# The scale of a finished stage and its first two splits placed ahead of the weights' steps of its last unit

## Chip, cores and metric

One Trainium2 chip, one of its cores. The metric is the device time of one execution in microseconds; three executions of the kernel before took 1237.06, 1237.91 and 1239.82 us, median 1237.91.

## What is computed

Attention over 4 batches and 12 heads (448 tokens, head size 64), whose output, 1792 tokens of 768 features, goes through two feed-forward blocks:

```python
q_n, k_n = rmsnorm(q, g_q), rmsnorm(k, g_k)
attn = softmax(scale * q_n @ k_n.T)
x = attn @ v                       # as [1792, 768]
x = (x @ w_a) * (x @ w_b) @ w_out  # 768 -> 1536 -> 768
h = x @ w_in                       # 768 -> 2048
out = (max(h, 0) + alpha * min(h, 0)) @ w_out2
```

All inputs are f32 drawn from a normal distribution; w_a, w_b, w_out and w_in, w_out2 are the weights of the two blocks.

## The kernel before

The batches go through four stages each: `a` (both products of the first block and their elementwise product `ab`), `y` (its output), `h` (the first product of the second block, with its activation) and `o` (the output). The stages are emitted in a fixed order: a0 y0 h0 o0 a1 y1 a2 h1 o1 y2 a3 h2 y3 o2 h3 o3. Every f32 operand of a product is split into two f16 parts, hi and lo, after a scaling by a power of two; a product is three matmuls (hi hi, hi lo, lo hi), `prod`. A stage is a run of units. A unit is one chain of matmuls against one weight tile of 128 columns: a stage `a` has 24 units of 18 matmuls (6 k-tiles), `y` 12 of 18, `h` 16 of 18, `o` 24 of 12. Between the units a stage yields, and steps of the attention of later batches are emitted there, at a rate for each stage.

The weights of the first batch are prepared while they are first used, in units numbered along the stream of the stages (a0 is 0 to 23, y0 24 to 35, h0 36 to 51, o0 52 to 75). `next_w` (L735), called once for each unit u, gives out what is due then by `advance` (L722) and the list `STEPS` (L714): the load of unit u + 10 (`w_load`, a DMA on SP's queue, L629), the convert of u + 8 (`w_convert`: L645 on ACT, L648 and L651 on DVE, the squares L659 on ACT), the scale of u + 6 (`w_scale`: a total over the partitions on PE by a matmul with ones, L123, then small columns on DVE by `power`, L110: L115, L118, L121) and the split of u + 3 (`w_split`: hi by L706 on ACT, lo by L707 on DVE, and a store to a scratch tensor in HBM, L710). From a1 on the split weights are only loaded back from the scratch tensor, four units ahead (L625). `next_w` also takes one task of the list `tasks` if there is any.

At the end of a stage `a` the last `ab` (L783 on DVE, read from the chain's PSUM tile) is squared on ACT with its sum (L786); a total on PE over all twelve sums, a reduction on DVE (L131) and `power` give the scale `sab`; then the twelve `ab` tiles are split with it (`split`, L759: hi by L761 on ACT, lo by L762 on DVE). A stage `y` ends alike: the last y tile is copied out on ACT (L821) and squared (L822), six `norm` matmuls with a matrix of ones add the squares, a maximum on DVE (L830) and `power` give `sy`, and six tiles are split. Where the next stage uses these tiles (a0, a1, and y0), the splits are emitted at once; elsewhere (a2, a3, y1, y2, y3) they are put on the list `tasks`, one for each following unit. `after` (L803) decides that.

The program's order is not the order on the engines. A scheduler of the framework places every instruction on its engine's queue before the run: among the instructions that it takes to be ready it prefers the one that was emitted earlier. The queues themselves run in order on the chip.

PSUM tiles named `x` (totals, `norm`, the attention's output `x`) share one buffer. The attention's own instructions that stand near the ends of the stages are L418 (maximum of scores), L431, L435 (exponent), L450, L480 and L481 (probabilities split), L531 and L532 (output split), L386 and L387 (values split).

Of the kernel before, what the change touches and what calls it, by code (L numbers as in the profile page):

```python
# [19 lines left out]
def attention_gated_mlps_kernel(  # L20
# [19 lines left out]
    KD, KF, KF2 = DM // 128, DF // 128, DF2 // 128  # L40
# [28 lines left out]
    def slot32(name):  # L69
        return slot_p.tile([128, S], F32, tag="slot", name=name)  # L70
# [36 lines left out]
    def mm(o, a, b, first, last):  # L107
        nc.tensor.matmul(out=o, lhsT=a, rhs=b, start=first, stop=last)  # L108

    def power(total, s, i):  # L110


        n = total.shape[1]
        h = sm_p.tile([128, 4], I32, tag="pw", name="pw")[:, 0:n]
        nc.vector.tensor_scalar(  # L115
            h, total.bitcast(I32), 1, 0x7F800000, op0=ALU.logical_shift_right, op1=ALU.bitwise_and
        )
        nc.vector.tensor_scalar(  # L118
            s.bitcast(I32), h, -1.0, float(205 << 23), op0=ALU.mult, op1=ALU.add
        )  # L120
        nc.vector.tensor_scalar(i.bitcast(I32), h, 1.0, float(49 << 23), op0=ALU.mult, op1=ALU.add)  # L121

    def total(cols, n, groups=1):  # L123

        ps = ps_x.tile([128, 512], F32, tag="x", name="tot")
        p = cols.shape[0]
        mm(ps[:, 0:n], ones[:p], cols, True, True)
        if n == groups:
            return ps[:, 0:n]
        t = sm_p.tile([128, 4], F32, tag="tot", name="tots")[:, 0:groups]  # L130
        nc.vector.reduce_sum(  # L131
            out=t, in_=ps[:, 0:n].rearrange("p (g k) -> p g k", g=groups), axis=AX.X
        )
        return t
# [476 lines left out]
    for st in stages:  # L611
        n, parts, _ = CHAINS[st[0]]
# [84 lines left out]
    def junk(width, n):  # L697
        return one_p.tile([128, width], BF16, tag="junk", name="junk")[:, 0:n]
# [23 lines left out]
    def advance(u):  # L722

        for todo, steps, done in ((firsts, STEPS, at[0]), (again, AGAIN, at[1])):
            for i, (f, ahead) in enumerate(steps):
                while done[i] < (done[i - 1] if i else len(todo)):
                    x = todo[done[i]]
                    if x > u + ahead or (f is w_split and x not in scales):
                        break
                    f(x)  # L730
                    done[i] += 1
# [3 lines left out]
    def next_w():  # L735
        u = cur[0]
        cur[0] += 1
        w16.pop(u)
        advance(u)
        if tasks:  # L740
            tasks.pop(0)()

    def unit():
        w = w16[cur[0]]
        return w.rearrange("p l (k f) -> p l k f", f=128)

    def prod(o, w, kk, x, first, last):
        hi, lo = w[:, 0, kk, :], w[:, 1, kk, :]
        mm(o, hi, x[:, 0], first, False)
        mm(o, hi, x[:, 1], False, False)  # L750
        mm(o, lo, x[:, 0], False, last)

    def new_ps():
        return ps_m.tile([128, 512], F32, tag="p", name="p")

    def tmp():
        return tmp_p.tile([128, S], F32, tag="t", name="t")

    def split(t, s, name):  # L759
        x = slot(name)  # L760
        nc.scalar.activation(out=x[:, 0], in_=t, func=AF.Copy, scale=s)  # L761
        nc.vector.scalar_tensor_tensor(  # L762
            out=x[:, 1], in0=t, scalar=s, in1=x[:, 0], op0=ALU.mult, op1=ALU.subtract
        )
        return x

    def stage_a(b):
        raw = {}
        for f in range(KF):
            for w in range(2):  # L770
                yield
                ps = new_ps()[:, 0:S]
                hw = unit()
                for kk in range(KD):
                    prod(ps, hw, kk, X[b, kk], kk == 0, kk == KD - 1)
                i = inv["a"][:, 2 * f + w:2 * f + w + 1]
                next_w()
                if w == 0:
                    t = tmp()
                    nc.scalar.activation(out=t, in_=ps, func=AF.Copy, scale=i)  # L780
                else:
                    raw[f] = ab = slot32(f"ab32_{b}_{f}")
                    nc.vector.scalar_tensor_tensor(  # L783
                        out=ab, in0=ps, scalar=i, in1=t, op0=ALU.mult, op1=ALU.mult
                    )
                    nc.scalar.activation(  # L786
                        out=junk(768, S), in_=ab, func=AF.Square,
                        accum_out=ssab[:, b % 2, f:f + 1],
                    )
        for kk in range(KD):  # L790
            X.pop((b, kk))
        power(total(ssab[:, b % 2], KF), sab[:, b:b + 1], iab[:, b:b + 1])

        def one(f):
            AB[b, f] = split(raw.pop(f), sab[:, b:b + 1], f"ab{b}_{f}")

        after(stages_after("a", b) == "y", one, KF)

    def stages_after(kind, b):
        i = stages.index(f"{kind}{b}")  # L800
        return stages[i + 1][0] if i + 1 < len(stages) and stages[i + 1][1] == str(b) else ""

    def after(now, one, n):  # L803
        if now:
            for i in range(n):
                one(i)
        else:
            tasks.extend((lambda i=i: one(i)) for i in range(n))

    def stage_y(b):  # L810
        raw, sq = {}, [slot_p.tile([128, 2, S], BF16, tag="slot", name=f"sq{b}_{i}") for i in range(KD // 2)]
        for m in range(KD):
            ps = new_ps()[:, 0:S]
            for kh in range(2):
                yield
                hw = unit()
                for kk in range(KD):
                    prod(ps, hw, kk, AB[b, kh * KD + kk], kh + kk == 0, kh == 1 and kk == KD - 1)
                if kh == 1:
                    raw[m] = t = slot32(f"y32_{b}_{m}")  # L820
                    nc.scalar.activation(out=t, in_=ps, func=AF.Copy, scale=inv["y"][:, m:m + 1])  # L821
                    nc.scalar.activation(out=sq[m // 2][:, m % 2], in_=t, func=AF.Square)  # L822
                next_w()
        for f in range(KF):
            AB.pop((b, f))
        ps = ps_x.tile([128, 512], F32, tag="x", name="norm")[:, 0:S]
        for m in range(KD):
            mm(ps, onesb, sq[m // 2][:, m % 2], m == 0, m == KD - 1)
        t = sm_p.tile([128, 1], F32, tag="mx", name="mx")
        nc.vector.tensor_reduce(out=t, in_=ps, axis=AX.X, op=ALU.max)  # L830
        power(t, sy[:, b:b + 1], iy[:, b:b + 1])

        def one(m):
            Y[b, m] = split(raw.pop(m), sy[:, b:b + 1], f"y{b}_{m}")

        after(stages_after("y", b) == "h", one, KD)

    def stage_h(b):
        raw = {}
# [79 lines left out]
    if True:  # L919
# [18 lines left out]
        n, done = 0, 0  # L938
# [18 lines left out]
        for i, st in enumerate(stages):  # L957
            s, b = st[0], int(st[1])
            if s == "a":
                while done < (b + 1) * NP:  # L960
                    step()
            n, parts, _ = CHAINS[s]
            ticks = n * parts
            gen = {"a": stage_a, "y": stage_y, "h": stage_h, "o": stage_o}[s](b)
            want, acc = 3 * RATE.get(st, 0), 0
            for _ in gen:
                acc += want
                while acc >= ticks:
                    acc -= ticks
                    step()  # L970
# [30 lines left out]
```

## Time and profile before

| | |
|---|---|
| median of 3 executions | 1237.91 us |
| profiled execution, its time | 1242.48 us |
| profiled execution, its span | 1240.7 us |
| mean granted TensorE clock | 0.981 |
| busy share of the span: PE, DVE, ACT, POOL | 94%, 55%, 60%, 1% |
| end of the last chain of a0, start of the first of y0 | 214.7 and 224.0 us |
| end of the last chain of y0, start of the first of h0 | 275.8 and 288.0 us |
| stretch read for h0, for o0 | 288 to 354 us, 354 to 444 us |

Times in the rows are microseconds from the start of the span. PE is TensorE's matmuls, whose ends are modelled; DVE is VectorE, ACT is ScalarE, SPq the DMA issues of SyncE. The first matmul of y0 comes 9.3 us after the last one of a0, the first of h0 12.2 us after the last one of y0; between them PE runs totals, `norm` and scores of the attention.

### The profile page before, as it was taken

Reading aid. Unit: us, or ns where it says so; the run is one execution under the profiler, and the core shown is the slowest. Engines: PE = TensorE matmul, PEld = TensorE weight load, DVE = VectorE, ACT = ScalarE, POOL = GpSimd, SP = SyncE. Lnnn points to the kernel's source line nnn. Section 1 sums busy time; section 2 is a strip of 40 time slices with the busy share of each in tenths; the row PEclk is TensorE's granted clock in tenths of the full one; section 3 lists DMA queues with packets and bytes.
Section 4 is the critical chain, followed back from the end, with each engine's and each line's share of the span. In section 5 each row is a group of like instructions: output and inputs, shape, how many; then the busy total and the mean of one; then the engine's idle time right before and its main releaser. Section 6 shows DMA issues by size and latency. Waiting matters only on the chain.

```text
span 1240.7 us, 18165 instructions
## 1 busy us (share of the span) xinstructions
PE 1169.5 (94%) x6574; PEld 598.9 (48%) x6574; DVE 679.8 (55%) x1455; ACT 740.8 (60%) x1504; POOL 9.2 (1%) x32
## 2 busy tenths in 40 slices
PE   6897998889999799989999999999999999999998
PEld 3553554444444444434455454545555555555554
DVE  7988998979999766677651466332111440102400
ACT  6998999989999966677642465543311441213311
POOL 1000000000000000000000000000000000000000
PEclk9997999897999999999999999999999999999999
DMA  6546999999999999987953737876333333344343
GB/s 185 172 139 184 287 323 306 297 277 306 302 269 300 268 258 243 228 189 183 213 160 115 177 117 164 187 190 164 102 115 115 115 115 110 106 143 131 98 126 90
DMA packets 311242, 234.67 MB, mean 189 GB/s; under 512 B 175440, under 2 KB 284496, under 8 KB 311152
## 3 DMA queue, kind: packets, MB, share of 16 engines
q1 hardware_dynamic: 311040, 233.43, 71.2%
q8 instruction: 52, 0.85, 0.3%
q0 software_dynamic: 112, 0.07, 0.1%
q14 instruction: 38, 0.31, 0.1%
HBM read 155.79 MB, written 32.24 MB: 152 GB/s over the span
## 4 chain that ended last, share of the span: by engine, by line
PE 53%; ACT 1%; DMA 1%; DVE 0%; issue 0%; SPq 0%; ACTq 0%
PE p L108 48%; PE s L108 2%; PE x L108 2%; DMA pT<-p 1%; PE p L884 1%; ACT t L877 0%; ACT pf L435 0%; PE norm L108 0%; ACT p L480 0%; DVE nm L418 0%; SPq L487 0%; DVE p L481 0%; ACT x L531 0%; PE tot L108 0%; DVE v L387 0%
## 5 line engine op out<-in xcount | busy, mean ns | idle before, releaser
L108 PEld LDWEIGHTS <-w 128*128 128x128 f16 x4896 | 475.9, 99 | 473.3 <-issue 45.3
L108 PE MATMUL p<-x,w 128*128 128x448 f16 x1728 | 335.9, 353 | 2.8 <-ACT t L780 2.0
L108 PE MATMUL p<-g,w 128*128 128x448 f16 x1152 | 230.0, 356 | 5.8 <-ACT w L706 2.5
L108 PE MATMUL p<-y,w 128*128 128x448 f16 x1152 | 223.3, 355 | 0.0
L108 PE MATMUL p<-ab,w 128*128 128x448 f16 x864 | 169.6, 356 | 1.7 <-ACT ab L761 1.6
L418 DVE TENSOR_REDUCE nm<-s 128x2 f32<-128x896 f32 x84 | 91.0, 1085 | 38.0 <-PE s L108 37.6
L480 ACT ACTIVATE p<-pf,ri 128x448 f16<-128x448 f32 x126 | 81.8, 663 | 35.3 <-DMA pT<-p 27.6
L108 PE MATMUL s<-kT,qT 128*64 128x448 f16 (+1 forms) x336 | 89.2, 433 | 14.1 <-ACT pf L435 10.3
L481 DVE SCALAR_TENSOR_TENSOR p<-pf,ri,p 128x448 f16<-128x448 f32 x126 | 84.4, 681 | 32.9 <-ACT p L480 32.7
L435 ACT ACTIVATE pf<-s,nm,esc 128x448 f32<-128x448 f32 x126 | 90.0, 718 | 1.3
L859 DVE SCALAR_TENSOR_TENSOR t<-t,al,p 128x448 f32<-128x448 f32 x55 | 37.3, 678 | 95.0 <-ACT t L858 95.0
L783 DVE SCALAR_TENSOR_TENSOR ab<-p,inv_a,t 128x448 f32<-128x448 f32 x48 | 32.6, 678 | 95.5 <-PE p L108 95.4
L707 DVE SCALAR_TENSOR_TENSOR w<-wf,sc,w 128x768 f16<-128x768 f32 (+1 forms) x76 | 70.0, 928 | 5.6 <-ACT w L706 5.3
L877 ACT ACTIVATE t<-p,inv_o 128x448 f32<-128x448 f32 x24 | 25.5, 1063 | 77.3 <-PE p L108 77.3
L645 ACT ACTIVATE wf<-raw 128x768 f32<-128x768 f32 (+1 forms) x76 | 63.1, 831 | 13.0 <-DMA raw<-in_moe_w_in_dram 5.4
L786 ACT ACTIVATE junk<-ab 128x448 bf16<-128x448 f32 x48 | 27.4, 571 | 68.1 <-DVE ab L783 68.0
L651 DVE SCALAR_TENSOR_TENSOR wf<-raw,wf 128x768 int32<-128x768 int32 (+1 forms) x76 | 66.0, 869 | 0.4
L706 ACT ACTIVATE w<-wf,sc 128x768 f16<-128x768 f32 (+1 forms) x76 | 65.0, 863 | 0.7 <-issue 0.7
L659 ACT ACTIVATE junk<-wf 128x768 bf16<-128x768 f32 (+1 forms) x76 | 58.9, 775 | 4.1 <-DVE sc L118 1.2
L858 ACT ACTIVATE t<-p 128x448 f32<-128x448 f32 x55 | 29.8, 541 | 46.8 <-PE p L108 46.4
L844 ACT ACTIVATE g<-t,cgf 128x448 f16<-128x448 f32 x55 | 36.7, 668 | 34.6 <-DVE t L859 34.6
L845 DVE SCALAR_TENSOR_TENSOR g<-t,cgf,g 128x448 f16<-128x448 f32 x55 | 37.5, 682 | 29.5 <-ACT g L844 29.5
(139 smaller groups left out, 1029.1 us busy)
## 6 DMA issues: line engine op xcount, KB each, us to landing
w<-sc_a SPq DMA_DIRECT2D x72, 384.0 KB, 3.1
w<-sc_h SPq DMA_DIRECT2D x48, 384.0 KB, 3.0
w<-sc_o SPq DMA_DIRECT2D x72, 256.0 KB, 3.1
w<-sc_y SPq DMA_DIRECT2D x36, 384.0 KB, 3.1
raw<-in_moe_w_in_dram SPq DMA_DIRECT2D x16, 768.0 KB, 7.3
raw<-in_moe_w_out_dram SPq DMA_DIRECT2D x24, 512.0 KB, 5.5
raw<-in_moe_w_a_dram SPq DMA_DIRECT2D x12, 768.0 KB, 7.0
raw<-in_moe_w_b_dram SPq DMA_DIRECT2D x12, 768.0 KB, 6.5
```

Of the source, the lines that this page charges most:

```text
L108: nc.tensor.matmul(out=o, lhsT=a, rhs=b, start=first, stop=last)
L418: nc.vector.tensor_reduce(out=nm, in_=ps[:, :, 0:S], axis=AX.X, op=ALU.max, negate=True)
L435: nc.scalar.activation(out=pf, in_=ps[:, j, 0:S], func=AF.Exp, bias=nm[:, j:j + 1], scale=scale[j], accum_out=su[:, j:j + 1],)
L480: nc.scalar.activation(out=t[:, 0, :, 0:KP], in_=pf, func=AF.Copy, scale=r)
L481: nc.vector.scalar_tensor_tensor(out=t[:, 1, :, 0:KP], in0=pf, scalar=r, in1=t[:, 0, :, 0:KP], op0=ALU.mult, op1=ALU.subtract,)
L645: nc.scalar.activation(out=t, in_=hi.bitcast(F32), func=AF.Prelu, scale=2.0 ** -112, alpha=-(2.0 ** 32))
L651: nc.vector.scalar_tensor_tensor(out=ti, in0=lo, scalar=29, in1=ti, op0=ALU.logical_shift_right, op1=ALU.bitwise_or)
L659: nc.scalar.activation(out=junk(768, size(kind)), in_=t, func=AF.Square, accum_out=sums[0][:, j:j + 1])
L706: nc.scalar.activation(out=w[:, 0], in_=t, func=AF.Copy, scale=s)
L707: nc.vector.scalar_tensor_tensor(out=w[:, 1], in0=t, scalar=s, in1=w[:, 0], op0=ALU.mult, op1=ALU.subtract)
L845: nc.vector.scalar_tensor_tensor(out=x[:, 1], in0=t, scalar=cgf[:, f:f + 1], in1=x[:, 0], op0=ALU.mult, op1=ALU.subtract,)
L859: nc.vector.scalar_tensor_tensor(out=t, in0=t, scalar=al[:, f:f + 1], in1=ps, op0=ALU.mult, op1=ALU.add)
```

## The change

The last `next_w` of the stages `a` and `y` is no longer called after the unit's matmuls (in `a` that was ahead of the eviction of `ab`, in `y` behind the eviction and square of the last tile) but from `after`, that is behind the total and the scale. Where the splits are emitted at once, it is called between the second and the third of them; where they become tasks, just ahead of queueing them. The number of calls is the same, and no instruction is added or removed.

```diff
@@ stage_a
                 i = inv["a"][:, 2 * f + w:2 * f + w + 1]
-                next_w()
+                if f < KF - 1 or w == 0:
+                    next_w()
                 if w == 0:
...
-        after(stages_after("a", b) == "y", one, KF)
+        after(stages_after("a", b) == "y", one, KF, next_w)
@@
-    def after(now, one, n):
+    def after(now, one, n, last):
+
         if now:
             for i in range(n):
+                if i == 2:
+                    last()
                 one(i)
         else:
+            last()
             tasks.extend((lambda i=i: one(i)) for i in range(n))
@@ stage_y
                     nc.scalar.activation(out=sq[m // 2][:, m % 2], in_=t, func=AF.Square)
-                next_w()
+                if m < KD - 1 or kh == 0:
+                    next_w()
...
-        after(stages_after("y", b) == "h", one, KD)
+        after(stages_after("y", b) == "h", one, KD, next_w)
```

## Rows read from the trace of the kernel before

**Rows 1.** Stretches: start:end, length, busy us of each engine (instructions), granted clock, DMA.
```profile
214.70:224.00 9.30, 3.26 (x23) 2.15 (x23) 8.81 (x24) 8.15 (x17) 0.19 (x1) 0.84 0.99 223
...
275.80:288.00 12.20, 6.66 (x27) 2.65 (x27) 10.41 (x32) 9.71 (x22) 0.44 (x1) 0.63 1.15 333
288.00:354.00 66.00, 65.12 (x358) 32.87 (x358) 62.74 (x124) 61.78 (x123) 1.02 (x3) 0.96 1.08 297
354.00:444.00 90.00, 78.18 (x448) 37.59 (x447) 74.35 (x167) 78.46 (x170) 0.00 (x0) 0.96 1.10 275
```

**Rows 2.** Timeline of PE, a0 to y0: start, us, instruction, [idle before <-releaser].
```profile
211.17 3.58 PE L108 MATMUL p<-x,w 128*128 128x448 f16 x18
...
221.00 0.60 PE L108 MATMUL tot<-ssab,ones 128*128 128x12 f32 x2 [2.76 <-ACT junk L786]
...
224.03 1.28 PE L108 MATMUL p<-ab,w 128*128 128x448 f16 x3 [1.57 <-ACT ab L761]
```

**Rows 3.** Timeline of DVE, end of a0.
```profile
216.08 1.01 DVE L707 SCALAR_TENSOR_TENSOR w<-wf,sc,w 128x768 f16<-128x768 f32 x1
...
217.67 0.55 DVE L648 TENSOR_SCALAR wf<-wf 128x768 int32<-128x768 int32 x1
...
218.25 0.96 DVE L651 SCALAR_TENSOR_TENSOR wf<-raw,wf 128x768 int32<-128x768 int32 x1
...
219.20 0.68 DVE L783 SCALAR_TENSOR_TENSOR ab<-p,inv_a,t 128x448 f32<-128x448 f32 x1
```

**Rows 4.** Timeline of ACT, end of a0.
```profile
218.26 0.67 ACT L480 ACTIVATE p<-pf,ri 128x448 f16<-128x448 f32 x1 [0.16 <-DMA pT<-p]
...
219.31 0.84 ACT L659 ACTIVATE junk<-wf 128x768 bf16<-128x768 f32 x1 [0.38 <-DVE tots L131]
...
220.28 0.58 ACT L786 ACTIVATE junk<-ab 128x448 bf16<-128x448 f32 x1
...
222.34 0.89 ACT L645 ACTIVATE wf<-raw 128x768 f32<-128x768 f32 x1 [0.58 <-DMA raw<-in_moe_w_out_dram]
...
223.32 6.81 ACT L761 ACTIVATE ab<-ab,sab 128x448 f16<-128x448 f32 x12
```

**Rows 5.** Timeline of PE, y0 to h0.
```profile
279.30 0.58 PE L108 MATMUL tot<-ss,ones 128*128 128x2 f32 x2 [2.80 <-ACT junk L659]
...
280.69 2.42 PE L108 MATMUL norm<-sq,onesb 128*128 128x448 bf16 x6
...
287.48 0.58 PE L108 MATMUL tot<-ss,ones 128*128 128x2 f32 x2 [2.73 <-ACT junk L659]
```

**Rows 6.** Timeline of DVE, end of y0.
```profile
283.15 0.62 DVE L830 TENSOR_REDUCE mx<-norm 128x1 f32<-128x448 f32 x1 [0.40 <-PE norm L108]
...
284.82 0.55 DVE L648 TENSOR_SCALAR wf<-wf 128x768 int32<-128x768 int32 x1
...
285.39 0.15 DVE L115 TENSOR_SCALAR pw<-mx 128x1 int32<-128x1 int32 x1
...
285.45 0.95 DVE L651 SCALAR_TENSOR_TENSOR wf<-raw,wf 128x768 int32<-128x768 int32 x1
```

**Rows 7.** Timeline of ACT, end of y0.
```profile
283.18 0.90 ACT L645 ACTIVATE wf<-raw 128x768 f32<-128x768 f32 x1
...
283.97 1.23 ACT L480 ACTIVATE p<-pf,ri 128x448 f16<-128x448 f32 x2
...
285.08 0.30 ACT L431 ACTIVATE nm<-nm,esc 128x2 f32<-128x2 f32 x1
...
286.50 0.84 ACT L659 ACTIVATE junk<-wf 128x768 bf16<-128x768 f32 x1 [1.11 <-DVE r L264]
...
287.34 3.44 ACT L761 ACTIVATE y<-y,sy 128x448 f16<-128x448 f32 x6
```

**Rows 8.** Timeline of PE, a unit of o0.
```profile
428.64 0.55 PE L108 MATMUL p<-g,w 128*128 128x448 f16 x2 [2.32 <-ACT w L706]
```

**Rows 9.** DMA issues: instruction, count, KB each, us from issue to landing.
```profile
w<-sc_y SPq DMA_DIRECT2D x36, 384.0 KB, 3.1
```

## The prediction

> **What bounds the kernel now.** I read stretches first, cut at the two ends of stages that the change touches while weights are still being prepared [rows 1]. In the 9.3 us between the last product of a0 and the first of y0 PE is busy 3.26 us at a mean granted clock of 0.84, while ScalarE (ACT) is busy 8.15 and VectorE (DVE) 8.81; in the 12.2 us of y0/h0 it is PE 6.66 at 0.63, ACT 9.71, DVE 10.41. So at these two ends PE waits for a chain through ACT and DVE, and their queues are nearly full. In h0 all three are full (PE 65.12 of 66, ACT 61.78, DVE 62.74); in o0 none is.
>
> What stands in the two queues is the point, so the timelines by engine come next. At a0's end PE has finished its chain at 214.75 (211.17 + 3.58), but the product `ab` of that chain starts on DVE only at 219.20, its squares on ACT at 220.28, the total on PE at 221.00 after 2.76 us idle, and the first product of y0 at 224.03 after 1.57 more [rows 2 to 4]. At y0's end PE waits 2.80 us before one total of weights and 2.73 us before another, each for L659, the square in the weights' convert [rows 5]. The six `norm` matmuls there take 2.42 us, 0.40 each, where eighteen of a0 took 3.58, 0.20 each [rows 2, 5]: they run at the 1.2 GHz level.
>
> **Which steps are moved.** Weights are numbered along the stream: a0 is 0 to 23, y0 24 to 35, h0 36 to 51, o0 52 to 75. The last `next_w` of a0 is that of unit 23: load 33, convert 31, scale 29, split 26. That of y0 is unit 35: load 45, convert 43, scale 41, split 38. Counting L645 from the start, its 32nd (unit 31) falls between 216 and 218 and its 44th (unit 43) is the one at 283.18 [rows 7]. Splits 26 and 38 had run before these stretches, so in them the moved work is one convert and one scale each: on ACT L645 (0.9 us) and L659 (0.84, and 0.19 for its sum), on DVE L648 (0.55) and L651 (0.96), small columns, a total on PE; on SP one load and one store.
>
> The order on an engine is not that of the program: L707 at 216.08 is split 27, which the program gives out in y0, and it runs ahead of a0's last `ab` [rows 3]. A step that was ready early fills a hole whatever its place. So the change can only turn pairs of which both were ready, and I count no others.
>
> **a0 to y0.** DVE is held from 217.67 by L648 and L651 of unit 31 (0.55, 0.96), and `ab` starts at 219.20 [rows 3]. With the two behind it, it starts at 217.67 and ends at 218.35. Its square on ACT then finds L480 until 218.93 (218.26 + 0.67), and no longer L659 of unit 31, which stands between now: 220.28 - 218.93 = **1.35 us** [rows 4]. From there to the first matmul of y0 I leave the 3.75 us as they are. Bounds: nothing, if L645 of unit 32 is still ahead of the first split, since that one waited for its weights until 222.34 and ends 0.09 before the split at 223.32; 2.1 us, if instead L645 of unit 31, whose weights are there, fills that place and the 0.58 us of waiting close too [rows 4]. I take 1.35, the rows' own difference.
>
> **y0 to h0.** The maximum of `norm` ends at 283.77 (283.15 + 0.62), the first column of its scale runs at 285.39, and the first split at 287.34 [rows 6, 7]. Between stand L648 and L651 of unit 43 on DVE (0.55 ahead of that column, 0.95 behind it) and L659 of unit 43 on ACT, at 286.50, just ahead of the split. A further L707 on DVE there is split 40, which needs scale 41; that is moved too. With these gone the two columns, 0.15 each, are out before 285, and the floor is ACT's own L480 pair with L431 behind it, out at 285.4: 287.34 - 285.4 = **1.94 us**. Bounds: nothing, if another convert that is ready fills the place; 2.8 us, if L645 of unit 43 (0.90) no longer stands ahead of the L480 pair. The total of scale 41 leaves the PE queue ahead of `norm`; I count nothing for it, as the last `norm` needs the last square of y0, which ACT reaches behind converts that don't move. The clock: some 12 products of h0 run at 0.40 where 0.20 is the full pace; if the shorter gap brings the clock back sooner that is up to 2.4 us, and I take none, since no row shows how much shorter it must be.
>
> **The rest.** The splits from the third on: the twelve of a0 ran in one piece of 6.81 us [rows 4], and now a convert may stand between the second and third. Two pairs give PE six matmuls, 2.4 us at 0.40 each, and a convert holds ACT 1.9 and DVE 1.5 us. That covers it by 0.5 us; at the full pace (1.2 us of work) the cover is gone and each of the two ends stalls 0.7 us. At a1's end weights come back ready made (like the rows of `sc_y`, 3.1 us to landing), four units ahead, so a load issued as late as the whole hand-over still has three units of 3.58 us to land [rows 2, 9]: nothing. The ends of a2, a3, y1, y2 and y3 take the other branch, which calls `next_w` after the scale and ahead of the queued splits; it moves one such load, at nothing, and tasks are taken in the same order. On SP the loads 33 and 45 and the stores move at most past the next issues; their products are ten units away. POOL gets none of it, and nothing of POOL's is waited for there.
>
> **The sum**: 1.35 + 1.94 = 3.3 us. The profiled execution took 1242.48 us (span 1240.7), 4.6 above the median of the runs and above the slowest of them; against its own time that is 1239.2, against the median 1237.91 - 3.3 = **1234.6 us**, 0.27% faster. A measurement of this kernel tells some 0.2% (2.5 us) from no change.
>
> **Rivals.** *Given back in o0.* The weights' steps are not less, only later. In h0 ACT has 4.2 us and DVE 3.3 us of 66 left [rows 1], and in o0 PE already waits for a split, 2.32 us at one place [rows 8]. If PE comes to o0 3.3 us earlier and the splits don't, it waits there: 1237.9, or 1236.5 if 1.4 of it survive. For it: ACT at 94% and DVE at 95% in h0. Against: o0 has room (ACT 78.46 of 90). The Trainium skill, Perfetto Trace Analysis, section Identifying the Most-Contended Engine, finds the binding engine by occupancy, and for TensorE by its weight loads instead of its matmuls. By that rule ACT and DVE bind h0 and a mere change of order gives nothing there; the weight loads in that stretch, 32.87 of 66, agree that PE is not the fullest, but no row shows which of the three gives way.
>
> *The order doesn't turn.* Steps that are ready go first, as split 27 did [rows 3]; if `ab` and the columns were not ready when the converts were taken, the queues stay as they are: 1237.9, at most 1 us off.
>
> *Slower: the weights come late into o0.* Convert 43 was complete at about 287.5 (286.50 + 0.84 and 0.19). Behind two splits from 285.4 it starts after 286.5 and takes 0.9 + 1.5 + 1.0 = 3.4 us, to 290.0: 2.5 us late, and all converts behind it too. If h0, which is full, can't win that back, it comes out in o0, where PE waits for splits [rows 8], and what was gained at the two ends is waited for as well: 1237.9 + 2.5 = 1240.4, and 1241.3 if all 3.4 us are late. It decides when the lag is over what DVE has free in h0, 3.3 us. Against it: a convert may fill the wait for the scale, and then nothing is late.
>
> **How the numbers follow.** My forecast 0.48 (0.44 of it beyond 0.2%), given back 0.20, order unchanged 0.10, slower 0.22. So faster 0.44, same 0.34 (0.04 + 0.20 + 0.10), slower 0.22. The upper bounds of the forecast, 2.1 + 2.8 + 2.4, give 1230.6; the slower rival's far end is 1241.3. The range from 1230.0 to 1241.5 holds both, with little beside them, and leaves out a new order of the whole weights' part. The forecast's own range is 1230.6 to 1237.9.
>
> **What would show it.** In the changed profile: `ab` of a0's end on DVE without L648 and L651 just ahead of it, and the total on PE 1.4 us sooner after the last chain; no L659 between the columns of `sy` and the first split; from the last chain to the first product 8 us at a0/y0 instead of 9.3, and 10.3 at y0/h0 instead of 12.2; L761 in two pieces, with a convert between. It is wrong if these stretches keep their length, if PE waits inside the first chain after the second pair, or if h0 and o0 grow by what they lost.

## The result, and the profile after

The changed kernel took **1250.05 us** (median of 4 runs, 1248.04 to 1253.24), beside 1238.87 for the kernel before on the same chip: ratio 1.0094, 95% interval 1.0067 to 1.0122. It is slower by 0.9%, on the other side of the forecast and beyond its range. The profiled execution took 1253.24 us (span 1251.5), 10.8 more than the one shown of before. Lines behind the edit are shifted: L783, L786, L830, L844, L845 and L877 of before are L784, L787, L836, L850, L851 and L883 here.

The stretches first, cut at the first and last product of each stage as PE's timeline has them; columns as in [rows 1]. In the changed kernel they are a0/y0, y0/h0, h0, o0 and a1:

```profile
216.39:226.03 9.64, 3.38 (x24) 2.28 (x23) 9.30 (x21) 8.15 (x18) 0.19 (x1) 0.80 0.93 235
277.13:285.12 7.99, 3.94 (x24) 1.62 (x23) 6.83 (x25) 6.99 (x16) 0.25 (x1) 0.90 1.10 359
285.12:351.44 66.32, 64.46 (x342) 32.30 (x343) 62.11 (x121) 59.59 (x118) 1.93 (x3) 0.93 1.07 303
352.25:447.82 95.57, 80.43 (x454) 38.61 (x452) 77.10 (x174) 81.33 (x177) 0.00 (x0) 0.95 1.02 256
450.13:561.67 111.54, 105.59 (x636) 51.32 (x635) 76.16 (x161) 72.55 (x169) 0.00 (x0) 1.00 0.98 228
```

The last three of the kernel before, cut in the same way (its first two are in [rows 1], but for a few hundredths):

```profile
288.04:351.27 63.23, 62.35 (x341) 31.56 (x341) 59.97 (x120) 59.01 (x118) 1.02 (x3) 0.96 1.09 298
352.07:442.51 90.44, 78.91 (x452) 38.08 (x452) 76.28 (x170) 79.32 (x173) 0.00 (x0) 0.96 1.10 277
444.65:552.61 107.96, 105.16 (x635) 51.01 (x636) 75.32 (x161) 73.09 (x169) 0.00 (x0) 1.00 0.98 232
```

The gap y0/h0 fell by 4.2 us, more than twice what was forecast. a0/y0 grew by 0.4. Then h0 is 3.1 us longer, o0 5.1, a1 3.6 and y1 1.0, with the same work in each. PE's busy time grows by 2.1, 1.5 and 0.4 us in h0, o0 and a1 (the granted clock is 0.93 instead of 0.96 in h0 and 0.95 instead of 0.96 in o0), its idle time by 1.0, 3.6 and 3.2; in o0 that is from 90.44 - 78.91 = 11.5 us to 15.1. From y1's end on both kernels take the same time, within 0.6 us. Another 1.6 us of the 10.8 arose ahead of a0's end, where the two kernels have the same queues: so much is scatter of single executions. The loss, then, lies where the diff touches nothing. PE's timeline in the changed o0 shows for what it waits between 369 and 402 us (waits of over 0.4 us alone):

```profile
370.24 0.38 PE L108 MATMUL s<-kT,qT 128*64 128x448 f16 x2 [1.26 <-DMA kT<-k]
...
384.30 0.55 PE L108 MATMUL p<-g,w 128*128 128x448 f16 x2 [2.13 <-ACT w L706]
385.70 3.70 PE L108 MATMUL p<-g,w 128*128 128x448 f16 x10 [0.84 <-DVE w L707]
...
399.19 0.55 PE L108 MATMUL p<-g,w 128*128 128x448 f16 x2 [0.42 <-ACT w L706]
401.23 2.07 PE L108 MATMUL p<-g,w 128*128 128x448 f16 x10 [1.48 <-DVE w L707]
```

These five sum to 6.1 us and the six others of o0 to 8.5; those of the kernel before sum to 10.6. Between 380 and 402 the kernel before has no wait for `w` of over 0.3 us. Here the first products of units 60 and 64 wait for their splits. On ACT's timeline of the changed kernel the convert of unit 64, which stands ahead of the split of unit 60 (at 383.55), shows why at first sight:

```profile
379.89 0.67 ACT L645 ACTIVATE wf<-raw 128x512 f32<-128x512 f32 x1 [3.20 <-DMA raw<-in_moe_w_out_dram]
```

Its load is issued at 372.61 (before: 364.98), behind transposes and loads of the attention on SP's queue; this is the timeline of SP, changed kernel:

```profile
363.55 1.35 SPq L352 DMA_TRANSPOSE qT<-q  x1
365.09 1.64 SPq L487 DMA_TRANSPOSE pT<-p  x1
366.78 1.32 SPq L355 DMA_TRANSPOSE kT<-k  x1
368.19 1.26 SPq L487 DMA_TRANSPOSE pT<-p  x1
...
372.09 0.48 SPq L207 DMA_DIRECT2D qr<-in_q_dram  x1
372.61 0.43 SPq L629 DMA_DIRECT2D raw<-in_moe_w_out_dram  x1
```

And these are late because attention is. The copies and subtractions that make the next head group's q and k halves stand in h0 in the kernel before (timelines of ACT and DVE):

```profile
321.89 0.57 ACT L342 CAST q<-qr 128x448 f16<-128x448 f32 x1
...
336.35 0.67 DVE L353 TENSOR_TENSOR k<-kr,k 112x512 f16<-112x512 f32 x1
```

and in the changed kernel 27 to 31 us later, in o0:

```profile
353.20 0.56 ACT L342 CAST q<-qr 128x448 f16<-128x448 f32 x1
...
362.92 0.68 DVE L353 TENSOR_TENSOR k<-kr,k 112x512 f16<-112x512 f32 x1
```

None of these instructions is named by the diff. The scheduler has made the queues anew: from a0's end to 511 us, in the middle of a1, another instruction stands at 444 places of PE's queue, 442 of DVE's, 317 of ACT's and 70 of SP's; behind that nothing differs. With the edit made at the ends of a1, a2, a3, y1, y2 and y3 alone, no place differs at all. So the whole result comes from the edit at the ends of a0 and y0.

### The profile page after: what moved, and what is told of

The parts are those of the page before. It is cut to its first block, busy times and chain, and to the rows that moved or that the text cites. A ratio compares the mean times of both kernels' runs of the same rounds, so it can differ in the third digit from the quotient of the medians.

```text
span 1251.5 us, 18153 instructions
## 1 busy us (share of the span) xinstructions
PE 1169.9 (93%) x6574; PEld 600.2 (48%) x6574; DVE 681.1 (54%) x1455; ACT 740.6 (59%) x1504; POOL 9.9 (1%) x32
## 4 chain that ended last, share of the span: by engine, by line
PE 52%; ACT 1%; DMA 1%; DVE 0%; issue 0%; SPq 0%; ACTq 0%
PE p L108 48%; PE s L108 2%; PE x L108 2%; DMA pT<-p 1%; PE p L890 1%; ACT t L883 0%; ACT pf L435 0%; PE norm L108 0%; DVE nm L418 0%; ACT p L480 0%; SPq L487 0%; DVE p L481 0%; ACT x L531 0%; PE tot L108 0%; DVE v L387 0%
## 5 line engine op out<-in xcount | busy, mean ns | idle before, releaser
L435 ACT ACTIVATE pf<-s,nm,esc 128x448 f32<-128x448 f32 x126 | 90.1, 718 | 1.4
L784 DVE SCALAR_TENSOR_TENSOR ab<-p,inv_a,t 128x448 f32<-128x448 f32 x48 | 32.6, 679 | 93.5 <-PE p L108 93.4
L883 ACT ACTIVATE t<-p,inv_o 128x448 f32<-128x448 f32 x24 | 25.6, 1066 | 78.8 <-PE p L108 78.8
L645 ACT ACTIVATE wf<-raw 128x768 f32<-128x768 f32 (+1 forms) x76 | 63.2, 833 | 15.2 <-DMA raw<-in_moe_w_out_dram 6.3
L787 ACT ACTIVATE junk<-ab 128x448 bf16<-128x448 f32 x48 | 27.4, 572 | 67.0 <-DVE ab L784 66.8
L651 DVE SCALAR_TENSOR_TENSOR wf<-raw,wf 128x768 int32<-128x768 int32 (+1 forms) x76 | 66.0, 870 | 0.5
L659 ACT ACTIVATE junk<-wf 128x768 bf16<-128x768 f32 (+1 forms) x76 | 59.0, 777 | 1.6 <-DVE pw L115 1.2
L850 ACT ACTIVATE g<-t,cgf 128x448 f16<-128x448 f32 x55 | 36.7, 668 | 34.6 <-DVE t L865 34.6
L851 DVE SCALAR_TENSOR_TENSOR g<-t,cgf,g 128x448 f16<-128x448 f32 x55 | 37.5, 683 | 29.5 <-ACT g L850 29.5
```

What stands on the lines that cost most here:

```text
L435: nc.scalar.activation(out=pf, in_=ps[:, j, 0:S], func=AF.Exp, bias=nm[:, j:j + 1], scale=scale[j], accum_out=su[:, j:j + 1],)
L645: nc.scalar.activation(out=t, in_=hi.bitcast(F32), func=AF.Prelu, scale=2.0 ** -112, alpha=-(2.0 ** 32))
L651: nc.vector.scalar_tensor_tensor(out=ti, in0=lo, scalar=29, in1=ti, op0=ALU.logical_shift_right, op1=ALU.bitwise_or)
L659: nc.scalar.activation(out=junk(768, size(kind)), in_=t, func=AF.Square, accum_out=sums[0][:, j:j + 1])
L851: nc.vector.scalar_tensor_tensor(out=x[:, 1], in0=t, scalar=cgf[:, f:f + 1], in1=x[:, 0], op0=ALU.mult, op1=ALU.subtract,)
```

## The experiments

Most kernels below hold each engine's queue to an order written into them: a list, and a dependency without a semaphore between neighbours. With the list of the kernel before in place every queue has the same instructions and waits as without it, so the list itself costs nothing, and pieces of one kernel's order can be put into the other's.

```diff
+def pin_order(tc, nc):
...
+            if was is not None:
+                tc.add_manual_dep(
+                    i, was.name,
+                    mybir.DependencyInfo(mybir.DependencyClass.NoSync, mybir.DependencyReason.DATA),
+                    reason="order",
+                )
+            was = i
...
         attention_gated_mlps_kernel(tc, *args)
+        pin_order(tc, nc)
```

All results in one table. Ratios are to the kernel before on the same chip, with the 95% interval; the last five columns are us of the one profiled execution, read off PE's timeline from last product to last product (y0/h0: last of y0 to first of h0). The stretch up to a0's end, where all these kernels have the same queues, took 212.6 to 216.4 us in them: a microsecond or two in one column can be chance.

| kernel | ratio | a0 to y0 end | y0/h0 | y0 to h0 end | h0 to o0 end | o0 to a1 end |
|---|---|---|---|---|---|---|
| before | 1 | 61.1 | 12.2 | 75.5 | 91.2 | 110.1 |
| changed | 1.0094 (1.0067 to 1.0122) | 60.7 | 8.0 | 74.3 | 96.4 | 113.9 |
| ends | 1.0028 (1.0009 to 1.0047) | 61.9 | 7.3 | 75.8 | 88.7 | 111.5 |
| later | 1.0082 (1.0056 to 1.0108) | 60.2 | 11.2 | 73.7 | 96.9 | 113.4 |
| o0only | 1.0076 (1.0048 to 1.0105) | 60.8 | 11.4 | 74.0 | 98.5 | 110.8 |
| sp_before | 1.0181 (1.0152 to 1.0211) | 61.0 | 8.0 | 75.3 | 101.0 | 118.6 |
| end_a0 | 1.0010 (0.9992 to 1.0028) | 63.7 | 9.3 | 72.7 | 89.8 | 112.6 |
| end_y0 | 1.0008 (0.9986 to 1.0031) | 60.3 | 7.4 | 74.7 | 89.0 | 108.3 |
| a1only | 1.0027 (1.0004 to 1.0050) | 60.4 | 11.0 | 73.6 | 90.9 | 115.6 |
| load64_early | 1.0068 (1.0041 to 1.0095) | 61.5 | 8.8 | 75.3 | 97.5 | 113.3 |
| load64_late | 1.0029 (1.0008 to 1.0049) | 60.8 | 11.9 | 75.3 | 92.5 | 108.7 |
| prep_load | 1.0051 (1.0033 to 1.0069) | 61.5 | 7.9 | 71.8 | 95.8 | 113.2 |
| prep_late | 1.0069 (1.0042 to 1.0096) | 60.3 | 11.5 | 74.1 | 100.0 | 108.5 |
| ab_first | 1.0063 (1.0041 to 1.0084) | 60.6 | 7.3 | 71.2 | 96.2 | 113.6 |
| a0 | 1.0074 (1.0055 to 1.0092) | 60.7 | 7.5 | 73.3 | 93.0 | 118.3 |
| y0 | 1.0077 (1.0057 to 1.0096) | 60.6 | 8.4 | 73.4 | 92.0 | 121.2 |
| cut0 | 1.0050 (1.0032 to 1.0068) | 60.7 | 7.4 | 71.4 | 99.4 | 111.2 |

### The ends against what follows: ends, later

`ends` has the changed kernel's order up to the first products of h0 and that of before from there on; `later` has it the other way round.

```diff
 ends:  PE places 0 to 1247, DVE 0 to 611, ACT 0 to 405
-       order of before
+       order of the changed kernel
 later: the places behind these, and SP's
-       order of before
+       order of the changed kernel
```

> The queues of PE, DVE and ACT stand as in the changed kernel through the ends of a0 and y0, up to some 292 us, and from there on, like SP's all along, exactly as in the kernel before. Theory A (the ends gain, and the loss comes from the other order that the scheduler gave the later steps): the 4 us gained at y0/h0 stay at least in part, 1235 to 1238 us. Theory B (the weights' steps, put behind the scale, are late themselves, whatever the order after them): 1247 to 1251 us. Theory C (what the ends gain is waited for again in h0 and o0, and the loss has another source): 1238 to 1240 us.

> The complement: the queues stand as in the kernel before through both ends, up to some 292 us, and from there on, with all of SP's, as in the changed kernel. Theory A: the whole loss and more, 1248 to 1254 us. Theory B: no loss, 1237 to 1241 us, since convert 31 and convert 43 stand where they did. Theory C: about the changed kernel's 1250 us, and never under it by more than 2.

`later` was 0.82% slower, nearly the whole loss, with both ends as before. `ends`, which has all that the diff asks for at both ends, the late converts included, was 0.28% slower, 2 us more than any theory of a kept or given-back gain allowed. In its profiled execution, the slowest of its ten, the gap y0/h0 is 7.3 us, and o0 is as short as any (88.7), but from y0's end to h0's end it needs 75.8 us, not less than the kernel before. So what the diff does at the ends doesn't pay, and causes at most the smaller part of the loss: 0.28% (0.09 to 0.47) of 0.94.

### Each end alone: end_y0, end_a0

```diff
 end_y0: PE places 1122 to 1247, DVE 562 to 611, ACT 371 to 405
 end_a0: PE places 895 to 987, DVE 478 to 561, ACT 302 to 370
-       order of before
+       order of the changed kernel
```

> The kernel before with the changed kernel's order of PE, DVE and ACT at the y0 to h0 end alone; the a0 end, o0 and a1 keep the order of before. Theory A (the y0 end keeps its gain): gap y0/h0 8 instead of 12.2 and h0 64 or less, median 1234 to 1237. Theory C (given back in h0, whose product chain waits for its weights and for attention): h0 67 to 68.5, median 1238 to 1240. A loss beyond that would say that the two ends run that cost 0.3% owes its loss to this end: 1241 or more.

> The kernel before with the changed kernel's order at the a0 to y0 end alone; all else as before. If the two ends cost 0.28% together and the y0 end 0.08%, this end costs about 0.2%: ratio 1.001 to 1.004, gap a0/y0 9.3 to 9.8. If it costs nothing by itself: 0.999 to 1.001 with the gap at 9.2. The forecast was a gain of 1.35 us here: 0.9985 to 0.9995.

Each by itself can't be told from the kernel before. The a0 end alone has none of the forecast 1.35 us: its gap a0/y0 is 9.7 instead of 9.3. The y0 end alone (median 1241.15 of 12 runs, beside 1240.31) missed the expected 1234 to 1237: in its profiled execution, the fastest of the twelve, its gap is 4.8 us shorter and h0 4.0 longer. These are the stretches of `end_y0` from y0's last product to h0's first, and h0:

```profile
272.88:280.30 7.42, 3.72 (x25) 1.61 (x23) 6.54 (x25) 6.66 (x16) 0.25 (x1) 0.98 1.10 359
280.30:347.55 67.25, 63.35 (x342) 32.79 (x343) 64.17 (x127) 62.34 (x125) 1.03 (x3) 0.95 1.09 304
```

Taken together the two have DVE busy 70.7 of 74.7 us (6.54 + 64.17) and ACT 69.0. The kernel before has for the same two together, as one stretch:

```profile
275.81:351.27 75.46, 69.04 (x366) 34.21 (x368) 70.42 (x151) 68.75 (x139) 1.47 (x4) 0.91 1.10 304
```

DVE's 70.42 us are the same work, and its share is 93 to 95% either way. PE came to h0 earlier and waited there instead, at two places of PE's timeline of `end_y0` that the kernel before hasn't (L870 is the activation of h on DVE):

```profile
293.83 3.56 PE L108 MATMUL p<-y,w 128*128 128x448 f16 x18 [1.50 <-DVE g L870]
...
310.28 1.27 PE L108 MATMUL x<-pT,v 112*64 112x448 f16 x7 [2.39 <-DVE pw L115]
```

`ends` has the same two waits in h0, 1.50 and 2.98 us, both for DVE.

### h0 and o0 alone, SP's queue alone: o0only, sp_before

`o0only` is the kernel before with the changed order in h0 and o0. `sp_before` is the changed kernel with the order of before on SP's queue alone.

```diff
 o0only:    PE places 1566 to 1870, DVE 612 to 888, ACT 406 to 623, SP 191 to 303
-       order of before
+       order of the changed kernel
 sp_before: all of SP
-       order of the changed kernel
+       order of before
```

> The kernel before, with the order of the changed kernel in h0 and o0 alone (292 to some 434 us on DVE and ACT, 310 to 443 on SP, the products of o0 on PE); both ends and a1 as before. Theory A with o0's order as the main cause: o0 some 95.5 us long instead of 90.4 and the time 1243 to 1246 us; a1 adds the rest in the changed kernel. Theory B: 1238 to 1240 us. If a1's own order were the only cause: 1238 to 1240 us as well, with o0 at 90 to 91 us.

> The changed kernel with the queue of SP alone in the order of the kernel before (PE, DVE and ACT as in the changed kernel). In the changed kernel load 64 stands behind three transposes, is issued at 372.6 instead of 365.0 and ACT waits 3.2 us for it. If that place in SP's queue is the cause of o0's loss: 1244 to 1247 us, 3 to 5 less than the changed kernel, and the wait of L645 near 380 us gone. If the order on ACT and DVE is the cause: 1249 to 1252 us.

`o0only` is 0.76% slower, more than was expected, and in its profiled execution all of that lies between h0's end and o0's (98.5 us); on PE the last six units of o0 keep the old order in it. `sp_before` was a miss: it loses 1.81%, twice what the changed kernel loses. An order on SP fits the orders on the other engines with which it was made; the old one by itself is no cure. Whether the changed order on SP alone costs the kernel before anything wasn't run.

### What in o0: load64_early, load64_late, prep_load, prep_late

First the load of unit 64, by one move on SP, in both directions:

```diff
 load64_early, on the changed kernel's SP:
 L710 DMA sc_o_3<-w                (unit 55)
+L629 DMA raw<-in_moe_w_out_dram   (unit 64)
 L352 DMA_TRANSPOSE qT<-q
...
 L207 DMA qr<-in_q_dram
-L629 DMA raw<-in_moe_w_out_dram   (unit 64)
 load64_late, on SP of the kernel before:
 L207 DMA qr<-in_q_dram
-L629 DMA raw<-in_moe_w_out_dram   (unit 64)
 L487 DMA_TRANSPOSE pT<-p
...
 L710 DMA sc_o_1<-w                (unit 57)
+L629 DMA raw<-in_moe_w_out_dram   (unit 64)
```

> The changed kernel with one instruction moved: on SP the load of unit 64's raw weights (o0) is issued right after the store of scale 55, ahead of two attention transposes of pT, those of qT and kT, the qS and the kr and qr loads; every other order is the changed kernel's. Theory T (in o0 the weights' chain runs late because this load lands at 379.9 instead of 371.3): o0 falls from 95.6 to about 91, the waits of 2.1 and 0.9 us at 384 to 386 and 1.5 at 401 go, median 1244 to 1246. Rival R (the late load is only a sign, the order of ACT, DVE and PE sets the pace): o0 stays above 94, median 1248 to 1252.

> The kernel before with one instruction moved: the load of unit 64's raw weights is issued behind two pT transposes and two scale stores, some 7 to 8 us later; nothing else differs. Theory T: PE gets waits on w around 384 and 401, o0 grows from 90.4 to 94 or 95, median 1242 to 1245. Rival R: the weights have enough lead, o0 stays at 90 to 91, median 1238 to 1240.

Early, the load lands at 368.92, and the waits before 384.30 and 385.70 go, as theory T has it. But o0 stays long, since the move has a cost of its own. At its new place the load waits on SP for 1.76 us, from 363.4 on, for DVE's L651, which reads a `raw` buffer, and the transposes of q and k stand behind it: the one that makes kT is issued at 368.45 instead of 366.78, as SP's timeline shows.

```profile
365.15 0.37 SPq L629 DMA_DIRECT2D raw<-in_moe_w_out_dram  x1
...
368.45 1.40 SPq L355 DMA_TRANSPOSE kT<-k  x1
```

On PE's timeline the wait for kT has grown from 1.26 to 2.68 us; the products of units 58 to 60 then run on without a break, and the wait of 1.5 us for `w` near 400 is that of the changed kernel:

```profile
372.27 0.38 PE L108 MATMUL s<-kT,qT 128*64 128x448 f16 x2 [2.68 <-DMA kT<-k]
...
379.49 7.01 PE L108 MATMUL p<-g,w 128*128 128x448 f16 x36
...
399.73 2.25 PE L108 MATMUL p<-g,w 128*128 128x448 f16 x11 [1.50 <-DVE w L707]
```

ACT, in order, meanwhile stands in a copy that waits for PE, so that the convert starts only 1.3 us earlier than in the changed kernel, though now without a wait for its load:

```profile
373.17 1.07 ACT L883 ACTIVATE t<-p,inv_o 128x448 f32<-128x448 f32 x1 [3.71 <-PE p L108]
...
378.59 0.67 ACT L645 ACTIVATE wf<-raw 128x512 f32<-128x512 f32 x1
```

So the first reading of ACT's row at 379.89 holds for the two waits at 384 to 386, but this run can't say what they cost o0, as the move put another wait in their place. In the kernel before, the same load 5.9 us later (issued 18.9 instead of 12.9 us after o0's first product; 7 to 8 were expected) made it 0.29% slower: there the load's place does count.

Then the attention's piece, put back early in the changed kernel together with that load, or put late in the kernel before:

```diff
 prep_load, on the changed kernel (prep_late the other way, on before):
 ACT
+L342 CAST q<-qr   (in h0)
+L344 CAST k<-kr
...
-L342 CAST q<-qr   (in o0)
-L344 CAST k<-kr
 DVE
+L350 TENSOR_TENSOR q<-qr,q
+L353 TENSOR_TENSOR k<-kr,k
...
-L350 TENSOR_TENSOR q<-qr,q
-L353 TENSOR_TENSOR k<-kr,k
 SP: the transposes qT and kT, two qS, kr and qr moved alike; the load of unit 64 in prep_load alone
```

> The changed kernel with one piece of attention put back to where the kernel before has it: the two ACT copies and two DVE subtractions that make the next head group's q and k halves, 20 to 25 us earlier, in h0; on SP its two transposes and two qS copies behind the stores of scales 52 to 54, then kr, qr and the load of unit 64 ahead of two pT transposes. All else is the changed kernel's. Theory L (in the changed order attention lags and its late transposes and that load hold ACT, and with it the weights of units 60 to 66): the wait for kT at 370 and ACT's wait of 3.2 us at 380 both go, the waits on w at 384 to 401 shrink from 4.9 us to under 2, o0 falls from 95.6 to 91 to 93, median 1245 to 1248. Rival M (the order of the weights' own steps costs it): o0 stays above 94.5 and the median at 1249 to 1252.

> The kernel before with one piece of attention late: the two ACT copies and two DVE subtractions of the next head group's q and k halves move from h0 (322 to 337 us) to 354 to 363 us, as the changed kernel has them, and its transposes and qS copies go behind the load of unit 63 on SP; the weights' loads keep their places. Theory L (this lag costs o0 its time): PE waits for kT near 368, o0 grows from 90.4 to 93 to 96, ratio 1.002 to 1.005. Rival M (the order of the weights' steps, not attention's lag, costs it): o0 90 to 92, ratio 0.999 to 1.001.

In `prep_late` these few instructions alone make the kernel before 0.69% slower, more than the expected 0.2 to 0.5, and o0 9 us longer: PE waits 6.28 us for kT, and 10.2 us around that wait are at the lower clock. PE's timeline of `prep_late`, and this stretch:

```profile
369.62 0.58 PE L108 MATMUL s<-kT,qT 128*64 128x448 f16 x2 [6.28 <-DMA kT<-k]
```

```profile
365.40:375.60 10.20, 4.91 (x15) 1.87 (x15) 4.38 (x9) 2.51 (x6) 0.00 (x0) 0.50 1.15 245
```

That is more than the changed kernel's own wait for kT, so it shows that the lag can cost as much, not that it does. The reverse says that it is not all: in `prep_load`, where ACT makes the copies at 338.6 (353.2 in the changed kernel, 321.9 in the kernel before), the waits for kT and at 380 to 386 are gone, and o0 is 95.8, hardly shorter, where 91 to 93 was expected. PE's timeline shows new waits in their place, and the old one at 397:

```profile
355.48 0.53 PE L108 MATMUL p<-g,w 128*128 128x448 f16 x1 [3.03 <-ACT g L850]
358.10 0.59 PE L108 MATMUL tot<-ss,ones 128*128 128x4 f32 x2 [2.09 <-ACT junk L659]
...
396.91 2.25 PE L108 MATMUL p<-g,w 128*128 128x448 f16 x11 [1.50 <-DVE w L707]
```

The ratio came down to 1.0051, in the direction expected; its interval and the changed kernel's still touch, so how much of it is the move stays open.

### a1: a1only, ab_first

```diff
 a1only:   PE from place 1995, DVE from 889, ACT from 624, SP from 304
-       order of before
+       order of the changed kernel
 ab_first, on the changed kernel's DVE at 520 us:
+L784 SCALAR_TENSOR_TENSOR ab<-p,inv_a,t
 L350 TENSOR_TENSOR q<-qr,q
 L353 TENSOR_TENSOR k<-kr,k
-L784 SCALAR_TENSOR_TENSOR ab<-p,inv_a,t
```

> The kernel before, with the changed kernel's order from the end of o0 on (a1 and y1) alone. Theory P (a1's new order itself costs, by waits of PE for the evictions ab): a1 111 to 112 instead of 108, median 1242 to 1245. Rival Q (a1 is long in the changed kernel because o0 hands it over late): a1 107 to 108, median 1237 to 1240.

> The changed kernel with one move on DVE in a1: the eviction ab of one product chain goes ahead of the two subtractions of q and k that stand before it at 520 to 522 us. Theory P (these hold the buffer that PE waits for): the wait of 2.5 us at 523 falls under 0.6, a1 from 111.5 to about 109.5, ratio about 0.0015 lower than the changed kernel's 1.0094. Rival Q (PE is then held by the next thing): a1 stays above 111.

`a1only` is 0.27% slower, as expected, with a1 longer than expected (114.0 us from its first product to its last, instead of 111 to 112). So a1's order costs by itself; it is not long only because o0 hands it over late. Its longest wait in the changed kernel, on PE's timeline, is this one:

```profile
523.42 3.56 PE L108 MATMUL p<-x,w 128*128 128x448 f16 x18 [2.51 <-DVE ab L784]
```

There the two kernels' queues are the same again (the last place that differs is at 511 us), so it is not the order at that place that costs. `ab_first` shows that it isn't one pair of instructions: this wait goes, and PE's timeline has two others in its place, with a1 itself at 111.9 instead of the expected 109.5. The ratio can't be told from the changed kernel's:

```profile
520.60 0.38 PE L108 MATMUL s<-kT,qT 128*64 128x448 f16 x2 [1.30 <-ACT pf L435]
522.27 3.56 PE L108 MATMUL p<-x,w 128*128 128x448 f16 x18 [0.73 <-ACT t L781]
```

### Other versions that the scheduler ordered itself: a0, y0, cut0

`a0` and `y0` make the change at one end only; `cut0` makes it everywhere, with the weights' steps ahead of all splits.

```diff
 a0 (y0 with "y0"):
+    MOVED = ("a0",)
...
-                if f < KF - 1 or w == 0:
+                if f < KF - 1 or w == 0 or f"a{b}" not in MOVED:
                     next_w()
 cut0:
-                if i == 2:
+                if i == 0:
                     last()
```

> The change at the end of a0 alone, as the program orders it by itself. Its queue orders differ from both kernels' from 219 us into a1, but attention's q and k halves of the next group stand about as early as before. Theory L: o0 88 to 92, so no loss there, median 1236 to 1241. Rival M (any new order of the weights' part is worse than the one before): o0 93 or more, median 1243 to 1250.

> The change at the end of y0 alone, as the program orders it by itself; q and k halves about as early as before. Theory L: gap y0/h0 8 instead of 12.2, h0 64 to 68, o0 88 to 92, median 1235 to 1241. Rival M: o0 93 or more, median 1243 to 1250.

> The change with the weights' steps ahead of all splits instead of behind the first two: the queue orders of h0, o0 and a1 are a third kind, with attention's q and k halves as late as in the changed kernel (50 places behind the split of unit 51 on DVE, where before has them 26 places ahead of it). Theory L: o0 94 to 98 as in the changed kernel, median 1245 to 1253. Rival M': without the two splits' head start the whole is back at the kernel before, 1238 to 1241.

All three are slower, by 0.50 to 0.77%, and not at the same place. In `a0` and `y0` the q and k halves stand early, and o0 is 2 to 3 us above the old order's mean of 89.9 (below): 93.0 and 92.0 from h0's end, 92.2 and 91.2 from its own first product, at the upper edge of the expected 88 to 92. But a1 is 8 and 11 us longer, PE waiting 3.15 and 4.56 us for one `ab`. In `cut0`, where DVE makes them late (at 356.8 and 357.4), it is o0 (99.4). The medians forecast for `a0` and `y0` were misses: a good o0 did not make a good kernel. `end_y0` and `y0` have the same edit; with all other places of the queues left as before it costs nothing that can be told, with the scheduler's own answer to it 0.77%.

## Why the prediction was wrong, point by point

**The account.** The table's columns can be grouped by whose order a kernel has in that stretch. Means of the profiled executions, with their extremes, of the kernels that share an order (`a0`, `y0`, `cut0`, `sp_before`'s later stages and those in which a single step was moved in the stretch have orders of their own):

- a0's end to y0's end: 60.6 with the old order of the a0 end (7 kernels, 60.2 to 61.1), 61.6 with the new (7, 60.6 to 63.7): **+1.0**, not clear of chance;
- y0's end to h0's end: 74.1 with the old y0 end (7, 72.7 to 75.5), 74.0 with the new (7, 71.2 to 75.8): **-0.1**, though the gap y0/h0 in it is 11.2 and 7.8;
- h0's end to o0's end: 89.9 with the old order (before, ends, end_a0, end_y0, a1only; 88.7 to 91.2), 97.0 with the changed kernel's (changed, later, o0only, ab_first; 96.2 to 98.5): **+7.1**;
- o0's end to a1's end: 110.1 with the old order (7; 108.3 to 112.6), 113.9 with the changed kernel's (changed, later, a1only, load64_early, prep_load; 113.2 to 115.6): **+3.8**.

Together 11.8 us, and the medians differ by 11.2 (1250.05 - 1238.87).

**The step that failed** is "So the change can only turn pairs of which both were ready, and I count no others", and with it the range, which "leaves out a new order of the whole weights' part". That split 27 ran ahead of a0's last `ab` [rows 3] was read as a sign that places move little. It said the opposite: the queues are made by a scheduler from when each instruction seems ready, so a few instructions elsewhere can shift what is ready next, and here the queues were laid out differently as far as the middle of a1, attention's steps among them. The terms at the two ends were then a sum over a few microseconds, and 7.1 + 3.8 = 10.9 us lay in o0 and a1, which had been put at nothing.

**a0 to y0, 1.35 us: not there.** The pair did not turn. DVE's timeline of the changed kernel still has unit 31's convert ahead of the last `ab`; [rows 3] show the same two lines:

```profile
219.34 0.56 DVE L648 TENSOR_SCALAR wf<-wf 128x768 int32<-128x768 int32 x1
219.93 0.96 DVE L651 SCALAR_TENSOR_TENSOR wf<-raw,wf 128x768 int32<-128x768 int32 x1
220.80 0.68 DVE L784 SCALAR_TENSOR_TENSOR ab<-p,inv_a,t 128x448 f32<-128x448 f32 x1
```

L659 of unit 31 did go behind the square, and the total came 0.35 us sooner after the chain (222.29 - 216.39 = 5.90, before 221.00 - 214.75 = 6.25). But then L431 and an L435 stand ahead of the first split besides the convert of unit 32, and the first product follows the total by 3.74 us instead of 3.03. So it is the rival that the order doesn't turn, for this end. (The upper bound of 2.1 us isn't the sum of its own terms: 1.35 + 0.58 = 1.93.)

**y0 to h0, 1.94 us: mechanism right, size 4.2, and given back.** L659 of unit 43 is behind the splits, as forecast; the convert's L645 still stands ahead of them. More was gained than was summed: the total of scale 41 went behind `norm`, which was put at nothing, and PE's stretch has the clock at 0.90 instead of 0.63 [rows 1]; five of the six `norm` products now run at 0.2 us each. ACT and PE of the changed kernel:

```profile
283.63 0.89 ACT L645 ACTIVATE wf<-raw 128x768 f32<-128x768 f32 x1
284.41 3.45 ACT L761 ACTIVATE y<-y,sy 128x448 f16<-128x448 f32 x6
...
289.38 0.84 ACT L659 ACTIVATE junk<-wf 128x768 bf16<-128x768 f32 x1
```

```profile
276.96 1.11 PE L108 MATMUL norm<-sq,onesb 128*128 128x448 bf16 x5
...
280.99 0.35 PE L108 MATMUL norm<-sq,onesb 128*128 128x448 bf16 x1 [2.04 <-ACT sq L827]
...
282.87 0.38 PE L108 MATMUL tot<-ss,ones 128*128 128x2 f32 x2
```

Behind the gap the clock gave nothing: it is at half from 283.6 to 290.4 us, and the first 14 products of h0 take 0.37 us each, as the first 12 do in the kernel before. Of the 2.4 us that the prediction left out for this nothing came.

None of the gain survived to h0's end. In h0 the changed kernel's longest wait is 1.86 us, where the kernel before waits 0.88 for the same instruction of the attention, L532, and behind it the clock is at half for 3.4 us, which it isn't there in the kernel before. PE's timeline of the changed kernel, then of the kernel before, then this stretch of the changed kernel:

```profile
319.87 0.38 PE L108 MATMUL tot<-ss,ones 128*128 128x2 f32 x2 [1.86 <-DVE x L532]
```

```profile
321.38 0.38 PE L108 MATMUL tot<-ss,ones 128*128 128x2 f32 x2 [0.88 <-DVE x L532]
```

```profile
321.10:324.50 3.40, 3.40 (x11) 1.42 (x10) 3.34 (x9) 3.12 (x7) 0.00 (x0) 0.50 1.09 250
```

The rival that it is given back was right in kind and wrong in place: it named o0, and it was h0, whose own fill (DVE at 95%) was quoted for it. The Trainium skill (Perfetto Trace Analysis, section Identifying the Most-Contended Engine) calls the engine with the highest occupancy the most contended one, and judges TensorE by its FLOPs or its weight loads instead of its matmuls' busy time. The trace agrees: over the stretch from y0's end to h0's in the kernel before DVE is the fullest, at 70.42 of 75.46 us (ACT 68.75, weight loads 34.21), and shortening PE's wait at its beginning moved its end by 0.1 us on the mean. That DVE alone sets this stretch isn't shown; ACT is only 1.7 us behind it.

**L761 in two pieces: wrong.** Both run without a convert between the second and third split; the scheduler took the splits first. So nothing stalled there either.

**The deferred ends and a1's hand-over: right at nothing.** The order behind a1 did not change, and the stages from a2 on take the same time.

**The slower rival: the right direction and the right stage, by another cause.** PE did wait for splits in o0. But by the rival's mechanism the late convert of unit 43 (complete 13.3 us after y0's last product instead of 11.7, so 1.6 us late where the rival had 2.5) should have carried its lag to o0, and `ends`, which has it at the same place of the queues, has one of the shortest o0 of all (88.7). With the order of before behind them, late converts are caught up.

**What stays open.** That the loss comes through the queue orders from h0 on, and falls in o0 and a1, is shown from both sides (`later` and `ends`). Which steps of these orders cost it isn't: each single move that was tried shifted the waits to other places. Where the 0.28% of `ends` goes isn't shown either. That the order of before is better than the four others because it was arrived at by trial is only a guess.

## What to carry to other kernels

Where a scheduler orders the queues by readiness, the first thing to compare is the queues themselves, and how far from the edit they differ: a forecast that sums the moved steps holds only for the part that stays in place. Hold the order of everything else fixed to measure an edit by itself, and ask of each gain whether the engine that is fullest over the whole stage, not the gap, has less to do. A wait that names one late DMA is tested by moving that DMA, and the move is read together with what it holds up: on an in-order queue a load that has to wait, as here 1.76 us for L651, delays all that is behind it.

## What the runs showed of the hardware

The granted clock fell to half inside o0, where PE otherwise works without long pauses. Before it fell PE had waited 2.13 and 0.84 us, until 384.30 and 385.70. Three stretches of the changed kernel, columns as in [rows 1]:

```profile
382.20:386.00 3.80, 0.85 (x4) 0.33 (x5) 3.80 (x10) 3.80 (x10) 0.00 (x0) 1.00 1.09 334
386.00:389.40 3.40, 3.40 (x12) 1.14 (x12) 3.40 (x9) 3.40 (x9) 0.00 (x0) 0.50 1.13 332
389.40:393.00 3.60, 3.60 (x25) 2.02 (x26) 3.30 (x8) 3.11 (x7) 0.00 (x0) 1.00 1.10 275
```

At the 1.2 GHz level PE runs 12 matmuls in 3.4 us, behind them 25 in 3.6 us (some of these smaller). By estimate, 3.4 us at half pace are 1.7 us of work lost on top of the waits. The changed kernel has three such stretches in o0 (from 358.7, 386.0 and 433.8 us) and one in h0 behind its first products (from 321.1), the kernel before two in o0 (from 361.0 and 429.2) and none in h0 behind its first products.

On SP's queue an issue of a transposing DMA holds what is behind it for longer than a load's: 1.26 to 1.64 us in the four rows of SP above, beside 0.43 and 0.48 for the two loads.
